# Attention over token chunks of 116 instead of 128 and 64, the first block of w_in in two halves, and a new written order of the first nineteen units

## The chip, the cores and the metric

The kernel runs on one core of one Trainium2 chip. The metric is the device time of one execution in microseconds. Each core has five engines that run their own instruction streams: TensorE (PE, with its weight loads PEld), VectorE (DVE), ScalarE (ACT), GpSimd (POOL) and SyncE (SP). SP issues most DMAs here; they run on 16 DMA engines.

## The reference

Two attentions and a feed-forward block. A short set of 32 packed queries `p` attends to 576 tokens; the result is the key and value of a second attention, whose output goes through a two-layer block with the activation `h * erf(softplus(h))`.

```python
batch, n_heads, seq, head_dim = (8, 8, 576, 64)      # 32 packed queries
def sm_attn(qq, kk, vv):
    s = scale * np.matmul(qq, kk.transpose(0, 1, 3, 2))
    s = s - np.max(s, axis=-1, keepdims=True)
    a = np.exp(s)
    a = a / (np.sum(a, axis=-1, keepdims=True) + 1e-09)
    return np.matmul(a, vv)
p_packed = sm_attn(p, k, v)
out = sm_attn(q, p_packed, p_packed)
# x: (4608, 512), heads side by side;  w_in: (512, 2048);  w_out: (2048, 512)
h = x @ w_in
sp = np.maximum(h, 0.0) + np.log1p(np.exp(-np.abs(h)))
g = h * erf(sp)
return (g @ w_out).astype(np.float32)
```

`w_in` and `w_out` arrive as 64-bit floats; the kernel takes their words apart itself.

## The kernel before

**Attention of a batch, `attention(b)`.** It is a generator: each `yield` ends a stage, and the caller decides where the next stage stands among the other work. The stages load `p` and four `k` tiles (line 233), then five `v` chunks of up to 128 tokens with all heads side by side (line 239: four of 128 rows and one of 64, 2,048 bytes a row), then four `q` tiles (244). First scores follow (252), their exponentials, the transposes of these token chunk by token chunk (`turn_chunks`, 267, and `turn_rest` for the last 64 tokens, 270), and the pooling `pool`, which multiplies each transposed chunk `a1t` with its chunk of `v` (277): two halves `r`, in each five chunks, in each four heads, so 40 products, which the trace counts as 80 matmuls. The pooled rows are normalised and transposed into `pt`. The second scores are `pt` against `q` (359), and their softmax over groups of 32 gives `a2`, kept as a high and a low part.

**The block.** The pooled values are multiplied into `w_in` once per batch: `w_prime(b, j)` (W, line 389) gives W' for the j-th 512 columns of `w_in`, in PSUM; `w_prime_high` (H on ScalarE, G on VectorE, 395) and `w_prime_low` (V, 400) keep it as two parts. A *unit* is 256 columns of the hidden layer for half a batch's tokens (288); there are 128 units. For each, `h_half` (h, 421) does six matmuls for 128 columns, `h_copy` takes them out of PSUM (c on ScalarE, d on VectorE, 429), `softplus` and `erf` (s, e) and `gate` (m, 443) form g, `split_high` (u on VectorE, U on ScalarE) and `split_low` (v) part it, and `o_part` (o, 472) multiplies with `w_out`; `put` (p, 481) writes results away.

**Weights.** A 512-column block of `w_in` is four tiles. `F j.c` issues the DMA of one of them (line 102, 4,096 bytes a row), `L j.c` writes the upper 16 bits (ScalarE, 108), `K j.c` merges the lower bits (VectorE, 112). `F f`, `L f`, `K f` do the same for a tile of `w_out`, and S or R (143) and T (146) split it. Staging tiles, `w_out` tiles and their splits share 18 buffers, tag `wo`.

**What sets the order.** The first part of the program is the string `BEGINNING`: words executed one after the other while the program is traced, and each engine's instructions (PE, DVE, ACT, SP) keep that order. `A`, `B` and `C` are the next stage of attention of batches 0, 1 and 2; `N` and `X` the next step of the second softmax of batch 0 for its first and second half of tokens; `i21` is 21 matmuls on an identity that keep PE's clock up. Units 0 to 3 and 4 to 7 belong to batch 0 (its two halves of tokens, first half of the hidden layer), 8 to 15 to batch 1, 16 to 19 to batch 0's second half of the hidden layer. From unit 20 a plan places the rest; attention of batch b+2 runs in pieces between the units of batch b.

Batch 0 has its own form (`roomy`): scores stay in PSUM, and `v` and `q` lie in buffers that are still free.

Of the kernel before, what the change touches and what calls it, by code (L numbers as in the profile page):

```python
# [26 lines left out]
BEGINNING = """
A A F0.2 F0.3 A F0.1 F0.0 i6 A A i9 A F3 F1.2 B F1.0 A A A F1.1 A F1.3 A A L0.2 K0.2 F2 A A A A A A A L0.1 L0.0 A F1
F2.1 A i21 N F5 N F0 N K0.1 B X N N L0.3 K0.3 N K0.0 N F7 N X F4 L1.2 K1.2 N N W0.0 H0.0 V0.0 B L3 B B B B X B L1.0 X
K1.0 h1.0 h1.1 c1.1 d1.0 F6 L1.1 K1.1 L1.3 K1.3 X h0.0 W0.1 G0.1 c0.0 L2 h0.1 V0.1 F2.0 d0.1 h3.0 h3.1 X X B B s1 X B  # L30
s0 e0 h2.0 e1 X X d2.0 h2.1 d2.1 d3.0 L0 L1 h4.0 h4.1 B c4.1 m0 K0 h5.0 h5.1 c5.0 L5 K1 B B d4.0 d5.1 s2 o0.3 K5 o0.2
L4 K3 c3.1 S0 m1 s3 o0.0 B s4 K2 e4 o1.0 L7 K4 B B e3 m4 R4 T0 K7 u4 m3 R1 T1 B B L6 K6 h6.0 h6.1 o0.1 o1.2 B B c6.1
o1.3 e2 m2 o1.1 c6.0 s5 B h7.0 h7.1 o2.0 S3 T3 o3.0 B B v4 R6 B e5 c7.1 S2 T2 B F8 o2.3 B c7.0 s7 o2.2 F2.2 L2.2 o3.3
p3.3 o2.1 o3.1 p3.1 p3.0 W1.0 o4.1 R7 s6 o4.3 B F3.1 L2.0 B B B B H1.0 o3.2 V1.0 F3.2 p3.2 m5 e7 o4.0 u5 v5 L2.1 K2.1
F2.3 L2.3 o4.2 h8.0 c8.0 m7 U7 K2.0 T7 F3.0 W1.1 G1.1 h9.0 c9.0 R5 T5 o5.3 K2.2 V1.1 T6 o5.0 K2.3 e6 m6 u6 T4 h8.1
o5.2 c8.1 s8 F11 h9.1 c9.1 s9 v6 o5.1 h10.0 c10.0 h10.1 c10.1 L3.0 F3.3 W0.2 v7 F9 s10 L8 e8 G0.2 V0.2 e10 m10 L3.2
L3.1 K3.1 m8 u8 v8 h11.0 h11.1 K3.2 L9 o6.0 o6.2 c11.1 e9 m9 c11.0 o6.3 o7.3 o6.1 F13 o7.1 o7.0 h12.0 h12.1 K3.0 o7.2
p7.1 L3.3 K3.3 u9 L11 v9 c12.0 p7.2 p7.0 h13.0 c12.1 s12 c13.0 s11 W0.3 G0.3 K8 h13.1 c13.1 F10 R8 T8 V0.3 o8.0 o9.0
o8.2 o9.2 o8.1 o9.1 p7.3 o8.3 s13 e13 F12 K9 S9 T9 e11 u10 m11 L10 h14.0 W1.2 v10 o10.2 K10 H1.2 S10 h14.1 V1.2 e12
d14.1 L12 o10.0 U11 F15 o9.3 T10 F14 c14.0 s14 K11 S11 v11 K12 R12 T12 W1.3 o10.1 H1.3 h15.0 T11 L14 h15.1 o10.3 o11.3  # L40
p11.3 m12 U12 c15.0 d15.1 s15 v12 o11.2 L13 o11.1 p11.1 o11.0 p11.0 h16.0 K14 K13 h16.1 c16.1 m13 S14 c16.0 s16 p11.2
R13 V1.3 u13 v13 e14 m14 o12.0 u14 h19.0 o12.1 d19.0 C T13 e15 v14 o12.3 o12.2 o13.2 h17.0 L15 e16 K15 o13.3 h17.1
c17.1 o13.0 C S15 d17.0 o13.1 o14.1 m15 s17 C h18.0 h18.1 u15 v15 C d18.0 h19.1 c19.1 T15 o14.3 s19 d18.1 o14.0 s18
e18 m16 e17 m17 T14 o14.2 e19 m19 C m18
"""


# [1 line left out]
def tile_pack_attention_moe(ctx: ExitStack, tc: tile.TileContext, qT, kT, v, pT, w_in, w_out, outT):  # L49
    nc = tc.nc  # L50
    P = 128
    B, _, NC, S = qT.shape
# [45 lines left out]
    def load_parts(src, name):

        n = src.shape[1]  # L100
        st = opool.tile([P, 4 * n + 2], U16, name=name, tag="wo")
        nc.sync.dma_start(st[:, 1:4 * n + 1], src.bitcast(U16))
        top = st[:, 2:4 * n + 2].bitcast(BF16).rearrange("p (n four) -> p n four", four=4)[:, :, 2]
        middle = st[:, 2:4 * n + 2].bitcast(U32).rearrange("p (n two) -> p n two", two=2)[:, :, 0]

        def land(dst):
            upper = dst.bitcast(F16).rearrange("p (n two) -> p n two", two=2)[:, :, 1]
            nc.scalar.copy(upper, top)  # L108

        def work(dst):  # L110
            bits = dst.bitcast(U32)
            nc.vector.scalar_tensor_tensor(bits, middle, 13, bits, op0=ALU.logical_shift_right, op1=ALU.bitwise_or)  # L112
# [87 lines left out]
    def attention(b):  # L200
# [34 lines left out]
        v_at = ("hs", "hs", "hs", "kvq", "kvq") if roomy else ("kvq",) * NCH  # L235
        values = [chunk(f"v{j}", v_at[j]) for j in range(NCH)]
        for j in range(NCH):
            n = min(P, S - j * P)
            nc.sync.dma_start(values[j][0:n, 0:2 * NC * 64], v[b, j * P:j * P + n, :])
# [31 lines left out]

        def pool(r, po):

            for j in range(NCH):
                n = min(P, S - j * P)
                for c in range(NC):
                    nc.tensor.matmul(po[NK * c:NK * c + NK, 64 * r:64 * r + 64],  # L277
                                     a1t[0:n, r, j, NK * c:NK * c + NK],
                                     values[j][0:n, 64 * (2 * c + r):64 * (2 * c + r) + 64],
                                     start=(r == 0 and j == 0), stop=(r == 1 and j == NCH - 1),  # L280
                                     skip_group_check=True)
# [101 lines left out]

    def w_prime(b, j):

        ps = ps_m.tile([P, 2, 512], F32, name=f"wp{b}_{j}", tag="ps_m")
# [4 lines left out]
        raw[b, j] = ps

    def w_prime_high(b, j, copy=nc.scalar.copy):
        hi = wpool.tile([P, 2, FB], F32R, name=f"wph{b}_{j}", tag="wph")
        copy(hi[:], raw[b, j][:])  # L395
        wp[b, j] = (hi, wpool.tile([P, 2, FB], F32R, name=f"wpl{b}_{j}", tag="wpl"))

    def w_prime_low(b, j):
# [1 line left out]
        nc.vector.tensor_tensor(lo[:], raw.pop((b, j))[:], hi[:], op=ALU.subtract)  # L400
# [301 lines left out]
```

## Time and profile before

| | |
|---|---|
| median of 3 runs | 734.68 us (734.39 to 735.19) |
| the profiled execution | 735.09 us |
| its span, first to last instruction | 733.3 us |
| granted TensorE clock, mean | 0.998 |
| PE, DVE, ACT busy | 98%, 75%, 78% of the span |
| moved by DMA | 58.42 MB |

A busy share is that of the whole span and mixes a start that waits for data with a long stretch in which PE has no gap; the stretches of time are therefore read one by one. A matmul's recorded time contains its way through the array, so sums of matmul times exceed what PE needs from start to start.

### The profile page before, as it was taken

The page shows a single profiled execution, that of the slowest core. Times are in us where ns is not written, and L with a number is a line of the kernel's source. Part 1 is how long each engine was busy: PE and PEld are TensorE (multiplying, and loading weights), DVE is VectorE, ACT ScalarE, POOL GpSimd, SP SyncE. Part 2 cuts the span into 40 slices and gives each one's busy share as a digit, 9 for nine tenths or more (in the row PEclk, how much of TensorE's full clock was granted, in tenths as well). Part 3 has the DMA queues.
Part 4 walks back from the last instruction along what each step waited for, and adds up shares of the span by engine and source line. Part 5 has one row for each costly group of instructions (what it writes and reads, how often), then busy time and mean ns, then how long its engine had stood idle before and what let it go on. Part 6 is the DMA issues. An engine that isn't in the chain of part 4 may idle for free.

```text
span 733.3 us, 15411 instructions
## 1 busy us (share of the span) xinstructions
PE 720.5 (98%) x6400; PEld 656.3 (89%) x6400; DVE 547.8 (75%) x831; ACT 573.0 (78%) x965; POOL 36.7 (5%) x56
## 2 busy tenths in 40 slices
...
GB/s 314 400 198 176 152 162 108 86 121 70 26 35 98 133 33 1 56 114 63 34 2 89 81 63 34 1 85 88 81 9 2 85 50 34 1 18 16 9 25 34
DMA packets 30279, 58.42 MB, mean 80 GB/s; under 512 B 3584, under 2 KB 12800, under 8 KB 30208
## 3 DMA queue, kind: packets, MB, share of 16 engines
...
## 4 chain that ended last, share of the span: by engine, by line
PE 88%; DMA 4%; DVE 4%; issue 1%; ACT 1%; SPq 0%; POOL 0%; POOLq 0%
PE o L472 54%; PE h L421 26%; PE wp L389 4%; DMA wos<-w_out 1%; PE p L277 1%; DMA wi<-w_in 1%; PE s L359 1%; PE s L252 1%; DMA k<-kT 1%; DMA v<-v 1%; PE t L267 1%; DVE gl L456 0%; DVE wohl L146 0%; DVE wpl L400 0%; ACT wo L108 0%
## 5 line engine op out<-in xcount | busy, mean ns | idle before, releaser
L472 PE MATMUL o<-gh,wohl 128*128 128x288 f32 x1984 | 422.7, 298 | 0.0
L472 PEld LDWEIGHTS o<-gh,wohl 128*128 128x128 f32 x1984 | 325.6, 188 | 13.7 <-issue 7.8
L472 PE MATMUL o<-gl,wohl 128*128 128x288 f32 x992 | 293.1, 296 | 0.1
L472 PEld LDWEIGHTS o<-gl,wohl 128*128 128x128 f32 x992 | 186.9, 188 | 0.9 <-DVE gl L456 0.4
L421 PE MATMUL h<-a2h,wph 128*128 128x288 f32 x512 | 154.3, 301 | 1.1 <-ACT hs L429 0.5
L421 PE MATMUL h<-a2h,wpl 128*128 128x288 f32 x512 | 151.6, 296 | 1.5 <-DVE wpl L400 1.5
L421 PE MATMUL h<-a2l,wph 128*128 128x288 f32 x512 | 151.0, 295 | 0.0
L431 ACT ACTIVATE hs<-h 128x288 f32<-128x288 f32 x192 | 77.9, 410 | 73.3 <-PE h L421 72.2
L519 DVE SCALAR_TENSOR_TENSOR hs<-t,hs 128x576 f32<-128x576 f32 x96 | 72.6, 756 | 62.6 <-ACT t L518 62.5
L421 PEld LDWEIGHTS h<-a2h,wph 128*128 128x128 f32 x512 | 96.1, 188 | 25.4 <-ACT u L515 8.4
L421 PEld LDWEIGHTS h<-a2h,wpl 128*128 128x128 f32 x512 | 96.0, 188 | 3.3 <-DVE wpl L400 2.4
L421 PEld LDWEIGHTS h<-a2l,wph 128*128 128x128 f32 x512 | 96.1, 188 | 0.9 <-issue 0.8
L456 DVE TENSOR_TENSOR gl<-hs,gh 128x576 fp32r<-128x576 f32 x124 | 93.5, 755 | 2.8 <-ACT gh L449 0.6
L518 ACT ACTIVATE t<-t,bias 128x576 f32<-128x576 f32 x96 | 74.0, 771 | 24.3 <-DVE t L517 24.3
L516 DVE SCALAR_TENSOR_TENSOR t<-t,hs 128x576 f32<-128x576 f32 x96 | 72.1, 751 | 17.3 <-ACT u L515 17.2
L449 DVE CAST gh<-hs 128x576 fp32r<-128x576 f32 x121 | 55.8, 461 | 31.3 <-PE o L472 28.1
L513 ACT ACTIVATE t<-hs,bias 128x576 f32<-128x576 f32 x96 | 74.6, 777 | 2.5
L515 ACT ACTIVATE u<-t,bias 128x576 f32<-128x576 f32 x96 | 74.5, 776 | 1.6
L514 ACT ACTIVATE t<-t,bias 128x576 f32<-128x576 f32 x96 | 74.2, 773 | 1.8
L517 DVE SCALAR_TENSOR_TENSOR t<-u,t 128x576 f32<-128x576 f32 x96 | 72.3, 753 | 1.4
L400 DVE TENSOR_TENSOR wpl<-wp,wph 128x1024 fp32r<-128x1024 f32 x32 | 38.8, 1211 | 7.0 <-ACT wph L395 6.2
L389 PE MATMUL wp<-w_in_sb,pt 64*32 64x512 f32 x512 | 37.1, 601 | 0.2 <-DVE w_in_sb L112 0.2
...
## 6 DMA issues: line engine op xcount, KB each, us to landing
k<-kT SPq DMA_DIRECT2D x32, 288.0 KB, 4.6
q<-qT SPq DMA_DIRECT2D x32, 288.0 KB, 4.2
v<-v SPq DMA_DIRECT2D x32, 256.0 KB, 3.6
wi<-w_in SPq DMA_DIRECT2D x16, 512.0 KB, 7.1
wos<-w_out SPq DMA_DIRECT2D x16, 512.0 KB, 6.5
...
v<-v SPq DMA_DIRECT2D x8, 128.0 KB, 4.0
```

Source lines behind the costliest of these rows:

```text
L389: nc.tensor.matmul(ps[NK * c:NK * c + NK, r, :], pt[b][64 * r:64 * r + 64, NK * c:NK * c + NK], w_in_sb[64 * r:64 * r + 64, c, j * FB:(j + ...
L421: nc.tensor.matmul(ps[:, 0:HT], w[:, r, fo:fo + P], a[:, r, c * HT:(c + 1) * HT], start=(m == 0), stop=(m == 5))
L431: nc.scalar.mul(dst, src, 0.5)
L456: nc.vector.tensor_tensor(glo[:], hs[:], ghi[:], op=ALU.subtract)
L472: nc.tensor.matmul(acc[b, c, d][:, 0:HT], w[f][:, d * P:(d + 1) * P], gg[:, k, :], start=(first and k == 0 and m == 0), stop=(last and k = ...
L513: nc.scalar.activation(t[:], hs[:], AF.Tanh, bias=bias[:, 0:1], scale=2.0 * T_SCALE)
L514: nc.scalar.activation(t[:], t[:], AF.Square, bias=bias[:, 1:2], scale=Q_SCALE)
L515: nc.scalar.activation(u[:], t[:], AF.Tanh, bias=bias[:, 2:3], scale=U_SCALE)
L516: nc.vector.scalar_tensor_tensor(t[:], t[:], 0.5 * A2, hs[:], op0=ALU.mult, op1=ALU.add)
L517: nc.vector.scalar_tensor_tensor(t[:], u[:], 0.5 * A1, t[:], op0=ALU.mult, op1=ALU.add)
L518: nc.scalar.activation(t[:], t[:], AF.Tanh, bias=bias[:, 3:4], scale=2.0 * A_SCALE)
L519: nc.vector.scalar_tensor_tensor(hs[:], t[:], 1.0, hs[:], op0=ALU.add, op1=ALU.mult)
```

## The change

Three things. First, the 576 tokens are cut into five chunks of nearly one size: four of 116 and one of 112. The loads of `v`, the transposes and `pool` go by these chunks; the transposed chunks keep their places, 128 columns apart. Second, block 0 of `w_in` can be loaded and used in two halves of 256 columns, named pieces 4 and 5: for batch 0, `F4.c`, `L4.c`, `K4.c`, `W0.4`, `H0.4`, `V0.4` and the same with 5 take the place of piece 0, with half the columns each. Both halves share one staging tile and one pair of W' tiles; a row of a half is 2,048 bytes. Batch 1 still forms W' of block 0 whole. Third, `BEGINNING` is written anew.

```diff
+    PIECES = [(j * FB, FB) for j in range(NFB)] + [(0, FB // 2), (FB // 2, FB // 2)]
-    NT = S // P
-    REM = S - NT * P
-    NCH = NT + 1
+    NCH = -(-S // P)
+    CH = -(-S // NCH // 4) * 4
+    NT = NCH - 1
+    REM = S - NT * CH
...
+    def load_w_in(j, c):
+        f0, n = PIECES[j]
+        dst, src = w_in_sb[:, c, f0:f0 + n], w_in[c * P:(c + 1) * P, f0:f0 + n]
...
+        if (f0 // FB, c) not in staged:
+            staged[f0 // FB, c] = staging(f"wi{j}_{c}", FB)
+        land, work = load_parts(staged[f0 // FB, c], src, f0 % FB)
...
-            n = min(P, S - j * P)
-            nc.sync.dma_start(values[j][0:n, 0:2 * NC * 64], v[b, j * P:j * P + n, :])
+            n = min(CH, S - j * CH)
+            nc.sync.dma_start(values[j][0:n, 0:2 * NC * 64], v[b, j * CH:j * CH + n, :])
...
-                nc.tensor.transpose(out[:, j * P:(j + 1) * P], a1[:, r, j * P:(j + 1) * P], ident[:])
+                nc.tensor.transpose(out[0:CH, j * P:(j + 1) * P], a1[:, r, j * CH:(j + 1) * CH], ident[:])
...
-            nc.tensor.transpose(out, a1[:, r, NT * P:S], ident[:])
+            nc.tensor.transpose(out, a1[:, r, NT * CH:S], ident[:])
...
-                n = min(P, S - j * P)
+                n = min(CH, S - j * CH)
...
-            nc.scalar.copy(a1t[:, :, 0:NT].rearrange("p r j k -> p r (j k)"), banks[:, :, 0:NT * P])
+            nc.scalar.copy(a1t[0:CH, :, 0:NT].rearrange("p r j k -> p r (j k)"), banks[0:CH, :, 0:NT * P])
...
+                nc.tensor.matmul(ps[NK * c:NK * c + NK, r, 0:n], pt[b][64 * r:64 * r + 64, NK * c:NK * c + NK],
+                                 w_in_sb[64 * r:64 * r + 64, c, f0:f0 + n], start=True, stop=True)
```

The start of the written order, before and after (the first three or so lines of each; F, L, K and A as above):

```diff
-A A F0.2 F0.3 A F0.1 F0.0 i6 A A i9 A F3 F1.2 B F1.0 A A A F1.1 A F1.3 A A L0.2 K0.2 F2 A A A A A A A L0.1 L0.0 A F1
-F2.1 A i21 N F5 N F0 N K0.1 B X N N L0.3 K0.3 N K0.0 N F7 N X F4 L1.2 K1.2 N N W0.0 H0.0 V0.0 B L3 B B B B X B L1.0 X
-K1.0 h1.0 h1.1 c1.1 d1.0 F6 L1.1 K1.1 L1.3 K1.3 X h0.0 W0.1 G0.1 c0.0 L2 h0.1 V0.1 F2.0 d0.1 h3.0 h3.1 X X B B s1 X B
+A A F5.2 F5.3 F4.2 A F4.1 F5.1 F4.0 F5.0 i6 A A A F4.3 i9 A A F3 F1.2 B F1.3 F1.0 F1.1 A A F2 A A A A L5.3 A L4.2 A A
+A K4.2 L5.2 K5.2 F5 A A L4.1 L5.1 F1 i21 A N F0 N N K5.1 K4.1 N N L4.0 F7 B L5.0 K4.0 L4.3 K4.3 W0.4 H0.4 N N N X V0.4
+K5.0 L1.2 N L3 K5.3 W0.5 B X B H0.5 B B B F4 N V0.5 h1.0 c1.0 L1.3 F2.1 K1.2 L1.0 h1.1 B L1.1 X X c1.1 h0.0 K1.0 K1.1
+K1.3 X W0.1 G0.1 F6 V0.1 c0.0 L2 h0.1 X h3.0 h3.1 d0.1 F2.0 X B B s1 B s0 e0 X X X h2.0 c2.0 h2.1 d2.1 d3.0 L0 B e1
```

In these lines the second `A` loads `v` of batch 0 and the third `A` its `q`; the first `B` loads `k`, the second `v` and the third `q` of batch 1. The rest of the string holds the same kinds of words in another order; over all of it, four more `h` copies stand on VectorE (17 d in place of 13), two fewer whole high parts of W' (2 G in place of 4), and one or two splits of `w_out` and of g changed engine.

More of the change, by code (lines that the diff above doesn't have):

```diff
@@ L27 @@
 BEGINNING = """
-A A F0.2 F0.3 A F0.1 F0.0 i6 A A i9 A F3 F1.2 B F1.0 A A A F1.1 A F1.3 A A L0.2 K0.2 F2 A A A A A A A L0.1 L0.0 A F1
-F2.1 A i21 N F5 N F0 N K0.1 B X N N L0.3 K0.3 N K0.0 N F7 N X F4 L1.2 K1.2 N N W0.0 H0.0 V0.0 B L3 B B B B X B L1.0 X
-K1.0 h1.0 h1.1 c1.1 d1.0 F6 L1.1 K1.1 L1.3 K1.3 X h0.0 W0.1 G0.1 c0.0 L2 h0.1 V0.1 F2.0 d0.1 h3.0 h3.1 X X B B s1 X B
-s0 e0 h2.0 e1 X X d2.0 h2.1 d2.1 d3.0 L0 L1 h4.0 h4.1 B c4.1 m0 K0 h5.0 h5.1 c5.0 L5 K1 B B d4.0 d5.1 s2 o0.3 K5 o0.2
-L4 K3 c3.1 S0 m1 s3 o0.0 B s4 K2 e4 o1.0 L7 K4 B B e3 m4 R4 T0 K7 u4 m3 R1 T1 B B L6 K6 h6.0 h6.1 o0.1 o1.2 B B c6.1
@@ L33 @@
[L33 to L42, printed above, removed]
@@ L43 @@
-c17.1 o13.0 C S15 d17.0 o13.1 o14.1 m15 s17 C h18.0 h18.1 u15 v15 C d18.0 h19.1 c19.1 T15 o14.3 s19 d18.1 o14.0 s18
-e18 m16 e17 m17 T14 o14.2 e19 m19 C m18
+A A F5.2 F5.3 F4.2 A F4.1 F5.1 F4.0 F5.0 i6 A A A F4.3 i9 A A F3 F1.2 B F1.3 F1.0 F1.1 A A F2 A A A A L5.3 A L4.2 A A
+A K4.2 L5.2 K5.2 F5 A A L4.1 L5.1 F1 i21 A N F0 N N K5.1 K4.1 N N L4.0 F7 B L5.0 K4.0 L4.3 K4.3 W0.4 H0.4 N N N X V0.4
+K5.0 L1.2 N L3 K5.3 W0.5 B X B H0.5 B B B F4 N V0.5 h1.0 c1.0 L1.3 F2.1 K1.2 L1.0 h1.1 B L1.1 X X c1.1 h0.0 K1.0 K1.1
@@ new lines @@
+K1.3 X W0.1 G0.1 F6 V0.1 c0.0 L2 h0.1 X h3.0 h3.1 d0.1 F2.0 X B B s1 B s0 e0 X X X h2.0 c2.0 h2.1 d2.1 d3.0 L0 B e1
+h4.0 L1 K0 h4.1 m0 h5.0 L5 B B d4.0 d4.1 s4 h5.1 c5.1 K1 o0.3 K3 K5 B s2 o0.2 L4 S0 d3.1 K2 s3 e4 m1 o1.2 e3 o0.0 o0.1
+o1.0 K4 B d5.0 B L7 m4 T0 K7 m3 R1 T1 B B L6 K6 h6.0 c6.0 h6.1 R4 c6.1 e2 S6 B B o1.1 m2 o1.3 B h7.0 h7.1 o2.0 S3 s5
+u4 e5 T3 B B v4 B R2 c7.1 T2 B B o2.3 o2.1 c7.0 s7 F2.2 o2.2 o3.3 L2.2 p3.3 s6 o3.1 p3.1 o3.0 p3.0 F3.1 B W1.0 H1.0 B
+B B R7 F3.2 L2.0 o3.2 p3.2 m5 U5 o4.3 V1.0 B v5 F2.3 K2.2 o4.0 e7 o4.1 L2.3 o4.2 W1.1 h8.0 d8.0 F3.0 m7 L2.1 K2.1 H1.1
@@ new lines @@
+V1.1 U7 e6 F8 m6 h9.0 d9.0 R5 o5.2 T5 o5.0 h8.1 o5.3 K2.3 K2.0 u6 c8.1 s8 h9.1 c9.1 T4 h10.0 c10.0 o5.1 s9 h10.1 v6
+c10.1 W0.2 T6 v7 L3.2 K3.2 F11 s10 F9 e10 L8 e8 L3.0 T7 G0.2 V0.2 m8 u8 L3.1 v8 h11.0 h11.1 c11.0 o6.2 d11.1 K8 K3.1
+o6.1 F13 e9 K3.0 L9 o6.0 o7.0 o6.3 o7.3 o7.1 h12.0 h12.1 K9 p7.0 o7.2 F3.3 L3.3 L11 K3.3 m9 u9 v9 c12.1 c12.0 p7.2
+h13.0 s12 s11 F12 W0.3 H0.3 h13.1 F10 m10 d13.0 d13.1 S8 T8 o8.2 o8.0 o9.0 p7.1 o8.1 s13 o9.1 h14.0 V0.3 S9 T9 o9.2
+e13 e11 m11 u10 p7.3 o8.3 L10 W1.2 K10 v10 L12 H1.2 o9.3 S10 V1.2 h14.1 d14.1 o10.0 e12 u11 F15 T10 F14 v11 K12 c14.0
@@ L45 @@
+s14 K11 R11 R12 o10.1 W1.3 H1.3 o11.0 h15.0 L14 T12 h15.1 o10.3 L13 o11.1 p11.1 o11.3 p11.3 T11 m12 U12 d15.1 d15.0
+s15 o10.2 h16.0 p11.0 h16.1 c16.1 o11.2 p11.2 K14 m13 v12 d16.0 s16 K13 R14 R13 u13 v13 o12.0 C e14 o12.1 h19.0 d19.0
+V1.3 T13 m14 e15 U14 m15 v14 L15 o12.3 K15 h17.0 h17.1 c17.1 e16 o12.2 o13.3 o13.0 o13.1 C h19.1 c19.1 S15 T15 o14.1 C
+h18.0 h18.1 c17.0 s17 c18.1 C o13.2 m16 o14.2 s19 c18.0 s18 e18 T14 U15 v15 e17 m17 e19 m18 m19 C o14.3 o14.0
 """
@@ L96, in tile_pack_attention_moe, with staging, load_parts @@
         nc.vector.memset(bias[:, i:i + 1], c)
[L98 to L104, printed above, removed]
+    def staging(name, n):
+        return opool.tile([P, 4 * n + 2], U16, name=name, tag="wo")
+    def load_parts(st, src, n0):
+        n1 = n0 + src.shape[1]
+        nc.sync.dma_start(st[:, 4 * n0 + 1:4 * n1 + 1], src.bitcast(U16))
+        words = st[:, 4 * n0 + 2:4 * n1 + 2]
+        top = words.bitcast(BF16).rearrange("p (n four) -> p n four", four=4)[:, :, 2]
+        middle = words.bitcast(U32).rearrange("p (n two) -> p n two", two=2)[:, :, 0]
         def land(dst):
@@ L114, in load_parts @@
         return land, work
-    def load_f32(dst, src, name):
-        if src.dtype == F32:
+    staged = {}
+    def load_w_in(j, c):
+        f0, n = PIECES[j]
+        dst, src = w_in_sb[:, c, f0:f0 + n], w_in[c * P:(c + 1) * P, f0:f0 + n]
+        if w_in.dtype == F32:
             nc.sync.dma_start(dst, src)
             return (lambda: None,) * 2
-        land, work = load_parts(src, name)
+        if (f0 // FB, c) not in staged:
+            staged[f0 // FB, c] = staging(f"wi{j}_{c}", FB)
+        land, work = load_parts(staged[f0 // FB, c], src, f0 % FB)
         return (lambda: land(dst)), (lambda: work(dst))
-    def load_w_in(j, c):
-        return load_f32(w_in_sb[:, c, j * FB:(j + 1) * FB], w_in[c * P:(c + 1) * P, j * FB:(j + 1) * FB], f"wi{j}_{c}")
     def load_w_out(f):
+        src = w_out[f * P:(f + 1) * P, :]
         if w_out.dtype == F32:
             wo[f] = opool.tile([P, DM], F32, name=f"wo{f}", tag="wo")[:]
-            return load_f32(wo[f], w_out[f * P:(f + 1) * P, :], f"wos{f}")
-        land, work = load_parts(w_out[f * P:(f + 1) * P, :], f"wos{f}")
+            nc.sync.dma_start(wo[f], src)
+            return (lambda: None,) * 2
+        land, work = load_parts(staging(f"wos{f}", DM), src, 0)
         def begin():
@@ L306, in attention @@
                 yield
-                copy(a1t[:, r, 0:NT].rearrange("p j k -> p (j k)"), turned[r][:, 0:NT * P])
+                copy(a1t[0:CH, r, 0:NT].rearrange("p j k -> p (j k)"), turned[r][0:CH, 0:NT * P])
                 copy(a1t[0:REM, r, NT], rest[0:REM, 0:P])
@@ L384, in w_prime @@
     def w_prime(b, j):
+        f0, n = PIECES[j]
         ps = ps_m.tile([P, 2, 512], F32, name=f"wp{b}_{j}", tag="ps_m")
```

16 lines of the change are left out of this document (9 added, 7 removed).

## The prediction, before the changed kernel was built

> **What bounds the kernel now.** I read the page first (busy shares, DMA issues), then busy time by stretches, then the chain of waits and the order of events of the first 60 us, last the pooling of one steady batch.
>
> ```profile
> span 733.3 us, 15411 instructions
> PE 720.5 (98%) x6400; PEld 656.3 (89%) x6400; DVE 547.8 (75%) x831; ACT 573.0 (78%) x965; POOL 36.7 (5%) x56
> ...
> q<-qT SPq DMA_DIRECT2D x32, 288.0 KB, 4.2
> v<-v SPq DMA_DIRECT2D x32, 256.0 KB, 3.6
> wi<-w_in SPq DMA_DIRECT2D x16, 512.0 KB, 7.1
> ...
> v<-v SPq DMA_DIRECT2D x8, 128.0 KB, 4.0
> ```
> ```profile
> core 0: us, PE busy (x) PEld busy (x) DVE busy (x) ACT busy (x) POOL busy (x), PEclk, DMA share, GB/s
> 0.00:10.00 10.00, 5.20 (x52) 4.33 (x53) 4.87 (x10) 1.28 (x1) 4.17 (x8) 1.00 0.80 258
> 10.00:20.00 10.00, 8.14 (x143) 5.88 (x142) 4.88 (x14) 3.79 (x13) 0.00 (x0) 0.92 1.03 385
> 20.00:30.00 10.00, 9.01 (x90) 6.59 (x88) 9.12 (x17) 7.03 (x13) 1.05 (x2) 0.91 1.04 397
> 30.00:40.00 10.00, 8.45 (x59) 5.81 (x58) 9.30 (x17) 9.29 (x16) 1.05 (x2) 1.00 1.04 383
> 40.00:50.00 10.00, 10.00 (x133) 8.60 (x132) 8.97 (x19) 9.55 (x16) 1.79 (x3) 1.00 0.66 248
> 50.00:60.00 10.00, 10.00 (x79) 7.39 (x78) 8.30 (x15) 9.49 (x15) 0.77 (x1) 1.00 0.06 8
> ...
> 300.00:400.00 100.00, 100.00 (x909) 91.84 (x910) 77.50 (x117) 81.12 (x142) 0.00 (x0) 1.00 0.20 62
> ```
>
> There are two regimes. From about 80 us TensorE is never idle (100.00 of 100 us in 300 to 400), so a microsecond taken off PE there comes off the end. Before that PE starts little (52 to 143 matmuls in 10 us): DMA is saturated from 10 to 40 us (1.03, 385 GB/s), and from 20 us VectorE and ScalarE are over nine tenths busy. What arrives later there starts everything later.
>
> **The order of the start.**
>
> ```profile
> 3.07 2.58 SPq L239 DMA_DIRECT2D v<-v  x5
> 7.79 2.66 SPq L244 DMA_DIRECT2D q<-qT  x4
> ```
> ```profile
> 4.50 6.59 DMA v<-v
> ```
> ```profile
> DMA to landing us min/median/max: 7.0/7.1/7.3
> ```
> ```profile
> SPq L244 <- DMA v<-v: 1.3, 3, 0.7
> ```
> ```profile
> 13.31 1.73 PE L277 MATMUL p<-v,a1t 128*32 128x64 f32 x80
> 14.76 0.69 DVE L112 SCALAR_TENSOR_TENSOR w_in_sb<-wi,w_in_sb 128x512 uint32<-128x512 uint32 x1 [1.54 <-ACT w_in_sb L108]
> 16.02 0.29 DVE L344 TENSOR_TENSOR a<-p,sm 128x128 f32<-128x128 f32 x1
> 17.05 1.24 PE L359 MATMUL s<-q,pt 64*32 64x288 f32 x32 [0.35 <-ACT pt L351]
> 17.89 0.85 DVE L174 STREAM_TRANSPOSE ta<-s 128x288 f32<-128x288 f32 x2 [1.57 <-PE s L359]
> 21.23 0.78 ACT L108 CAST w_in_sb<-wi 128x512 f16<-128x512 bf16 x1 [0.53 <-DMA wi<-w_in]
> 24.79 0.75 DVE L187 TENSOR_TENSOR ta<-ta,mx 128x576 f32<-128x576 f32 x1
> 28.22 1.22 DVE L400 TENSOR_TENSOR wpl<-wp,wph 128x1024 fp32r<-128x1024 f32 x1
> 29.50 0.40 PE L421 MATMUL h<-a2h,wpl 128*128 128x288 f32 x1 [0.73 <-DVE wpl L400]
> ```
>
> These are, in this order: SP's issues, a piece of the chain of waits, the landing time of q's four transfers, SP's waits of the first 24 us, and the timeline. The fourth v chunk is issued at 4.50 and lands at 11.09. q lands 7.0 to 7.3 us after its issue, the last of which begins at 10.1 (7.79 + 2.66 less one issue), so it is complete at 17.1 to 17.4, beside the second scores at 17.05. The last piece of w_in's first block lands at 21.2 (ScalarE waits for it). From 17.89 VectorE works nearly without a gap to the low half of W' at 29.44, which releases the matmul at 29.50.
>
> **The change part by part.**
>
> *Pooling on TensorE (gain).* One steady batch, loads alone:
>
> ```profile
> 235.12 1.73 PE L277 MATMUL p<-v,a1t 128*32 128x64 f32 x80
> 236.78 0.40 PE L472 MATMUL o<-gl,wohl 128*128 128x288 f32 x1
> ```
> ```profile
> 235.11:235.55 0.44, 0.43 (x32) 1.00 0.00 0
> 235.55:235.69 0.14, 0.06 (x5) 1.00 0.00 0
> 235.69:235.80 0.11, 0.10 (x8) 1.00 0.00 0
> 235.80:235.94 0.14, 0.06 (x8) 1.00 0.00 0
> ```
>
> Pooling lasts 1.66 us from its first start to that of the next matmul. In each half of it 32 loads of the 128-row form go in 0.44 us (0.11 per eight), then nothing new starts for 0.14 us until the array works in the 64-row form, eight go in 0.11, and again 0.14 pass. With chunks of 116 and 112 rows all ten sets have the long form (more than 64 rows don't fit the short one). Three of the four pauses go; the last, into the 128*128 matmuls, stays: 3 x 0.135 = 0.40 us a batch. Ends: 0 if every change of chunk pauses, 0.42. Six steady batches: 2.4 us off the end. Batches 0 and 1 lie in the start, where other work decides, so their 0.4 is not counted. The transposes keep their number, and the rest's (now 112 wide) its 128 moving columns: 0, at most 0.05 us a batch.
>
> *Loads of v (loss).* A chunk is 128 rows of 2,048 bytes, eight to each of 16 DMA engines; the 64-row chunk is four each and lands no sooner (4.0 against 3.6 us). 116 = 4 x 29 has no equal share for 16. No row shows such a transfer. Bounds: shares of eight and seven, as the 128-row row (cost 0); or equal shares on four engines, 29 rows each. (One engine would have no reason, since four divides.) The ends are far apart. I take the equal deal, because each transfer in this trace divides by 16 and none shows an uneven one; both ends stay in the range. The Trainium skill, "DMA: Bandwidth & Descriptors", section "Why a DMA increments its semaphore by 16 and not by 1", says that a transfer runs on the largest number of engines, up to 16, that divides the slowest dimension of both sides: four for 116, all 16 for 112. No run here shows it yet; by that rule the sum is the one that follows, without it the first rival's.
>
> One engine's rate is 385 / 16 = 24.1 GB/s. The busiest four carry 4 x 29 + 7 = 123 rows of v instead of 36: 87 x 2,048 bytes = 178 KB, 7.4 us. All that is queued after v on these four is late by that. v is complete near 11.5 + 7.4 = 18.9 instead of before the pooling at 13.31; pooling's second half (0.6) and the 2.0 us from its end at 15.04 to 17.05 give 21.5. q comes later: it goes behind three half pieces of w_in (768 KB, before 1,024: 0.7 us less), so 17.2 + 7.4 - 0.7 = 23.9. The second scores thus start 6.8 us late. The last half piece lands near 21.2 + 7.4 = 28.6; it is cast and merged by 29.4, and behind it on VectorE stand, up to W0.5's low part, five operations over 576 elements (0.75 to 0.85 each), a small reciprocal (0.4), two half merges and two half low parts (priced below), 6.6 us: 36.0, while 23.9 + 12.4 (17.05 to 29.44) gives 36.3. Both say 6.6 us after 29.44. The queue throttles further: each transfer waits for the landing of the one eight before it (q waits for v three times above), so q is issued one piece per late v chunk; it stays ahead of its place on the four engines, so I add 0. Idle PE can't make it up: VectorE and ScalarE are the limit until 80 us, and their work has only moved.
>
> *v of batch 1.* The same 7.4 us again.
>
> ```profile
> L277 PE MATMUL p<-v,a1t x80: 216/219/243, 47.7 to 49.3; 128*32 128x64 f32 x64, 64*32 64x64 f32 x16
> L239 SPq DMA_DIRECT2D v<-v x5: 328/328/471, 28.3 to 33.6; - x5
> ...
> DMA to landing us min/median/max: 7.8/8.9/10.2
> ```
>
> Landed by 43.8 at most, needed at 47.7. After: 43.8 + 14.8 = 58.6 against 47.7 + 6.6 = 54.3, so up to 4.3 us more; 0 if the landing is nearer the median and DMA's free time (0.66 and 0.06 in 40 to 60) takes it up. I take 2.3. The next batches are covered, and without cover would cost 7.4 each:
>
> ```profile
> L277 PE MATMUL p<-v,a1t x80: 216/219/243, 149.4 to 150.9; 128*32 128x64 f32 x64, 64*32 64x64 f32 x16
> L239 SPq DMA_DIRECT2D v<-v x3: 328/367/477, 131.3 to 132.2; - x3
> ```
>
> 17 us lie between issue and use.
>
> *Halves.* Four more DMAs, ScalarE casts and VectorE merges, one more W' with its high and low copy. VectorE: 0.75 us at 576 elements, 0.29 at 128, so 1.02 ns each and 0.16 fixed; a half merge is 0.42 against 0.69, a half low part 0.70 against 1.22. Between second scores and first finished W' there were three merges of block 0, one of block 1 and one low part (3 x 0.69 + 0.68 + 1.22 = 3.97); now six half merges and two half low parts (3.92). Equal: 0; ends -0.3 and +0.8, the latter if the four extra casts of ScalarE (0.78 whole, some 0.2 of it fixed) lie on the path. K0.2, which delayed pooling's sums (14.76 to 15.45), is split and stands elsewhere: under the late v, nothing.
>
> *Order.* On SP's queue F7 now goes ahead of batch 1's v and F2.1 behind its q (512 KB each: they cancel, 1.4 us either way). On the engines four `h` copies, two block copies and some splits change between ScalarE and VectorE, about 2 us in all; both are full from 20 to 80 us. I take 0, ends -1.5 and +1.5.
>
> **The sum.** Profiled execution 735.09 us (span 733.3 and 1.8 around it), which is 0.4 over the median of 734.68: 735.1 + 6.6 + 2.3 - 2.4 = 741.6, against the median 741.2; I say 741.
>
> **Rivals.**
> 1. *The 116 rows go to all 16 engines.* Then nothing is late, q even 0.6 earlier (three half pieces ahead of it instead of two whole ones), and the pauses' 2.4 us remain: 734.7 - 2.4 - 0.6 = 731.7 (730.4 to 733.2 with the order's ends). For it: the 64-row rows give no hint of a worse deal; against it: 116 / 16 is no whole number. It decides if v is complete by about 16 us. Faster.
> 2. *The start is late, but batch 1's v costs its full 4.3 us and ScalarE's half casts and the order 1.5 more:* 734.7 + 6.6 + 4.3 + 1.5 - 2.4 = 744.7. For it: 9.3 to 9.6 us of ScalarE's 10 in 30 to 50; against it: DMA's pause after 50 us.
> 3. *The late start is mostly absorbed*, because the new order does other work meanwhile: 2.4 us of loss would be left to cancel the gain, 734.7. Against it: that work needs the same late w_in pieces.
>
> **Numbers.** Equal shares on four engines with the cost as summed 0.60, rival 2 0.10, rival 1 0.25, rival 3 0.05. Likeliest case's own range: 737.3 (5.0 us at the start, none at batch 1) to 743.5. Since the faster case holds 0.25, the range goes to it: 730.5 to 745. A measurement tells 0.2% (1.5 us) from no change: faster 0.25, same 0.05, slower 0.70.
>
> **What would show it.** v's 116-row transfers of batch 0 land 3 to 8 us later than 11.1 and one after the other, some 2.4 us apart; pooling of batch 0 starts or ends near 19, second scores near 24, the first matmul with W' low near 36; GB/s in 10 to 20 us falls far under 385 while something still waits for DMA. A steady pooling lasts about 1.26 us with 128*32 forms alone. If v lands by 11 to 12 us, the forecast is wrong by its largest term; if pooling still takes 1.6, by its gain.

## The result

The changed kernel takes 745.21 us (median of 4 runs, 744.92 to 745.32), the kernel before 734.93 us beside it on the same chip: a ratio of 1.014, 95% interval 1.0122 to 1.0157. The change costs 10.3 us. The forecast was 741.0 with a range up to 745.0: the direction and the main mechanism were right, the size was 4.2 us short, and the time lies 0.2 us above the range.

First the page of the changed kernel: its span, the busy time, and the group of v's issues.

```profile
span 743.4 us, 15448 instructions
...
PE 721.6 (97%) x6416; PEld 657.2 (88%) x6416; DVE 545.1 (73%) x835; ACT 575.6 (77%) x971; POOL 36.2 (5%) x56
...
v<-v SPq DMA_DIRECT2D x32, 232.0 KB
```

The busy times are those of before within 3 us on every engine, so the 10 us are almost all waiting. Busy time by stretches (PE, PEld, DVE, ACT, POOL, then granted clock, DMA share, GB/s) says where:

```profile
10.00:20.00 10.00, 4.72 (x57) 3.04 (x55) 2.15 (x9) 2.79 (x10) 0.00 (x0) 0.78 0.72 200
20.00:30.00 10.00, 9.19 (x113) 6.39 (x114) 5.05 (x11) 4.16 (x10) 0.00 (x0) 0.71 0.95 313
30.00:40.00 10.00, 6.59 (x94) 4.80 (x93) 9.85 (x21) 6.87 (x15) 0.53 (x1) 1.00 1.02 400
40.00:50.00 10.00, 8.77 (x63) 6.59 (x64) 8.69 (x17) 9.37 (x16) 1.05 (x2) 1.00 0.75 256
50.00:60.00 10.00, 7.29 (x107) 5.79 (x106) 5.71 (x11) 5.23 (x9) 1.79 (x3) 0.83 0.85 263
...
300.00:400.00 100.00, 100.00 (x906) 92.60 (x902) 78.17 (x115) 80.38 (x136) 0.00 (x0) 1.00 0.15 49
```

From 10 to 20 us DMA moves 200 GB/s where it moved 385, while five chunks of v are waited for; VectorE works 2.15 of those 10 us (4.88 before), and the granted TensorE clock is 0.78 and then 0.71 (0.92 and 0.91 before). From 50 to 60 us the same comes again for batch 1: 5.71 against 8.30 on VectorE, and the clock falls to 0.83. The steady stretch has no gap, as before.

The start in the timeline (start, duration, idle time before it and what ended that; PEld is TensorE's weight load):

```profile
13.60 0.43 PE L286 MATMUL p<-v,a1t 116*32 116x64 f32 x16
16.80 0.44 PE L286 MATMUL p<-v,a1t 116*32 116x64 f32 x8 [2.77 <-DMA v<-v]
19.18 0.44 PE L286 MATMUL p<-v,a1t 116*32 116x64 f32 x8 [1.93 <-DMA v<-v]
20.04 1.51 PE L286 MATMUL p<-v,a1t 112*32 112x64 f32 x48 [0.42 <-DMA v<-v]
22.80 3.64 PE L368 MATMUL s<-q,pt 64*32 64x288 f32 x32 [0.36 <-ACT pt L360]
24.02 0.18 PEld L368 LDWEIGHTS s<-q,pt 64*32 64x32 f32 x4 [0.58 <-DMA q<-qT]
25.95 0.85 DVE L183 STREAM_TRANSPOSE ta<-s 128x288 f32<-128x288 f32 x2 [2.37 <-PE s L368]
35.96 0.69 DVE L416 TENSOR_TENSOR wpl<-wp,wph 128x512 fp32r<-128x512 f32 x1
36.71 0.40 PE L437 MATMUL h<-a2h,wpl 128*128 128x288 f32 x1
```

Two chunks are there at 13.60; the next two come at 16.80 and 19.18, 2.4 us apart, and the last, of 112 rows, at 20.04. The second scores start at 22.80 (17.05 before), VectorE begins on them at 25.95 (17.89), the first matmul with the low half of W' at 36.71 (29.50). The same for batch 1:

```profile
53.37 0.43 PE L286 MATMUL p<-v,a1t 116*32 116x64 f32 x16
53.95 0.32 PE L286 MATMUL p<-v,a1t 116*32 116x64 f32 x8 [0.15 <-DMA v<-v]
56.50 0.41 PE L286 MATMUL p<-v,a1t 116*32 116x64 f32 x8 [2.23 <-DMA v<-v]
57.24 1.51 PE L286 MATMUL p<-v,a1t 112*32 112x64 f32 x48 [0.33 <-DMA v<-v]
58.68 7.44 PE L488 MATMUL o<-hs,wo 128*128 128x288 f32 x20
```

The 20 `o` matmuls take 7.44 us here. In the kernel with chunks of 112 below they take 5.29. That row, and not only the waits above it, is what the forecast lacked. The pooling of a steady batch, last:

```profile
246.88 1.33 PE L286 MATMUL p<-v,a1t 116*32 116x64 f32 x80
248.13 0.40 PE L488 MATMUL o<-gl,wohl 128*128 128x288 f32 x1
```

From its first start to the next matmul 1.25 us pass, where before there were 1.66, and only the long array form is left.

### The profile page after: what moved, and what is told of

Its sections match the earlier page's. It is cut to its first block, busy times and chain, and to the rows that moved or that the text cites. A ratio compares the mean times of both kernels' runs of the same rounds, so it can differ in the third digit from the quotient of the medians.

```text
span 743.4 us, 15448 instructions
## 1 busy us (share of the span) xinstructions
PE 721.6 (97%) x6416; PEld 657.2 (88%) x6416; DVE 545.1 (73%) x835; ACT 575.6 (77%) x971; POOL 36.2 (5%) x56
## 4 chain that ended last, share of the span: by engine, by line
PE 93%; DMA 4%; DVE 2%; SPq 1%; ACT 0%; issue 0%
PE o L488 56%; PE h L437 27%; PE wp L399 5%; DMA v<-v 4%; PE s L368 2%; PE p L286 1%; PE s L261 1%; PE t L276 1%; DVE w_in_sb L117 0%; SPq L248 0%; SPq L242 0%; DVE ta L183 0%; DVE mx L185 0%; DVE ta L187 0%; DVE m L299 0%; PE p L279 0%
## 5 line engine op out<-in xcount | busy, mean ns | idle before, releaser
L534 ACT ACTIVATE t<-t,bias 128x576 f32<-128x576 f32 x96 | 74.0, 771 | 23.9 <-DVE t L533 23.8
L416 DVE TENSOR_TENSOR wpl<-wp,wph 128x1024 fp32r<-128x1024 f32 (+1 forms) x33 | 38.9, 1179 | 7.1 <-ACT wph L412 6.2
L399 PE MATMUL wp<-w_in_sb,pt 64*32 64x512 f32 (+1 forms) x528 | 37.5, 588 | 3.6 <-DVE w_in_sb L117 3.6
```

The source lines that it names most:

```text
L399: nc.tensor.matmul(ps[NK * c:NK * c + NK, r, 0:n], pt[b][64 * r:64 * r + 64, NK * c:NK * c + NK], w_in_sb[64 * r:64 * r + 64, c, f0:f0 + n ...
L534: nc.scalar.activation(t[:], t[:], AF.Tanh, bias=bias[:, 3:4], scale=2.0 * A_SCALE)
```

## Experiments

All times are medians beside the kernel before, which took 734.7 to 735.1 us in these comparisons; ratios are to it, with their 95% intervals.

### Which part of the change costs

**Chunks of 112.** The changed kernel with four chunks of 112 rows and one of 128, which both divide by 16.

```diff
-    CH = -(-S // NCH // 4) * 4
+    CH = 112
...
-            n = min(CH, S - j * CH)
+            n = CH if j < NT else REM
...
```

> The changed kernel with four chunks of 112 tokens and one of 128, all else as changed (halves, new order). Theory D (the deal: a v transfer runs on as many DMA engines as divide its rows, so 116 rows on four): all chunks divide by 16, batch 0's chunks land near 11 us as before the change, pooling of a steady batch stays at 1.26 us, total 731 us (730 to 733), PE's losses before 150 us at or under those of the kernel before. Rival O (the loss comes from the new order and the halves): over 742 us, second scores still near 23 us.

Measured 732.3 us, ratio 0.9964 (0.9951 to 0.9976): 12.9 us less than with 116, from four rows a chunk. The pooling and second scores of batch 0, and pooling of batch 1 with the `o` matmuls behind it, in its timeline:

```profile
13.88 1.40 PE L286 MATMUL p<-v,a1t 112*32 112x64 f32 x80
16.38 1.57 PE L368 MATMUL s<-q,pt 64*32 64x288 f32 x32 [0.35 <-ACT pt L360]
...
46.58 1.33 PE L286 MATMUL p<-v,a1t 112*32 112x64 f32 x80
47.84 5.29 PE L488 MATMUL o<-hs,wo 128*128 128x288 f32 x20
```

No wait for v stands before either pooling. This version beats both kernels.

**The kernel before with 116.** Its own order and whole pieces of w_in, chunks of 116 and 112.

```diff
-    NT = S // P
-    REM = S - NT * P
-    NCH = NT + 1
+    NCH = -(-S // P)
+    CH = 116
+    NT = NCH - 1
+    REM = S - NT * CH
...
```

> The kernel before, its order and whole w_in blocks kept, with chunks of 116 and 112 only. Theory D: v lands 2.4 us apart, second scores near 23.5 us, pooling of batch 1 waits for v again: 741 to 746 us. Rival O: 732.3 us, since only the pauses of steady pooling go.

Measured 747.43 us, ratio 1.0174 (1.0161 to 1.0188): the chunk alone brings the whole loss, 2.2 us more than in the new order and 1.4 us above what either theory allowed; why more was not taken apart.

**The kernel before with 112.** The same, with one number more.

```diff
-    CH = 116
+    CH = 112
```

> The kernel before with chunks of 112 and 128 only. Both theories: steady pooling 1.26 us in place of 1.66, six batches, so 734.8 - 2.4 = 732.4 us; another 0.4 if batch 0's shorter pooling counts at the start (731.9 to 732.6). If it is over 733.5, the gain of the pauses is partly lost again.

Measured 733.04 us, ratio 0.9974 (0.9963 to 0.9984): the pooling's gain alone, about 2 us.

**Halves and order alone.** The changed kernel with the old chunks of 128 and 64.

```diff
-    CH = -(-S // NCH // 4) * 4
+    CH = 128
...
```

> The changed kernel (halves and new order) with the chunks of the kernel before, 128 and 64. Theory D: the order and the halves are worth little, 733.3 to 735.5 us, pooling 1.66 us again. Rival O: 745.2 + 2.4 = 747.6 us.

Measured 734.31 us, ratio 0.9993 (0.9984 to 1.0002): with chunks that arrive in time, the two halves and the new order are worth nothing that can be measured.

### What 116 does to a load

**117 and 118 rows.** The same edit as for 112 with `CH = 117` and `CH = 118`: 117 = 13 x 9 and 118 = 2 x 59. If the rows are dealt out in equal shares, 117 goes to 13 engines and 118 to 2.

> The changed kernel with chunks of 117 tokens and one of 108. 117 = 13 x 9, 108 = 12 x 9. Theory D (equal shares on the largest number of engines up to 16 that divides the rows): 45 rows of v on the busiest engine instead of 36, so 0.8 us more per batch and no visible wait: 732 to 734 us, though 117 is no multiple of 16 nor even. Rival M (any transfer whose rows are no multiple of 16 is slow): 745 us or more.

> The changed kernel with chunks of 118 tokens and one of 104. 118 = 2 x 59. Theory D: two engines, 59 rows each, 4.9 us a chunk; busiest engine 249 rows instead of 36, that is 18 us late per early batch where 116 gave 7.4: 755 to 772 us, batch 0's chunks landing 4.9 us apart. Rival M: like 116, 745 us.

Measured 732.51 us (0.9971; 0.9961 to 0.998) with 117, 763.67 us (1.0397; 1.0376 to 1.0418) with 118. One row more than 116 removes the loss, two rows more make it more than twice as large. The pooling of batch 0, first with 117, then with 118:

```profile
13.77 1.40 PE L286 MATMUL p<-v,a1t 117*32 117x64 f32 x80
```
```profile
17.20 0.44 PE L286 MATMUL p<-v,a1t 118*32 118x64 f32 x8 [3.00 <-DMA v<-v]
23.26 0.44 PE L286 MATMUL p<-v,a1t 118*32 118x64 f32 x8 [5.62 <-DMA v<-v]
28.67 0.44 PE L286 MATMUL p<-v,a1t 118*32 118x64 f32 x8 [4.97 <-DMA v<-v]
```

Chunks of 118 arrive 5.4 to 6.1 us apart, those of 116 2.4 us apart. With equal shares that is 59 x 2,048 bytes in 5.4 to 6.1 us and 29 x 2,048 in 2.4 us: an estimate of 20 to 22 and of 25 GB/s for one engine, beside the 24.1 that the forecast took. That is the rule of the Trainium skill, "DMA: Bandwidth & Descriptors", section "Why a DMA increments its semaphore by 16 and not by 1", which the prediction cited without a run behind it; these three sizes agree with it.

**116 rows, loaded as 112 and 4.** Pooling computes on 116 rows, and each load is split into two DMAs.

```diff
-            nc.sync.dma_start(values[j][0:n, ...], v[b, j * CH:j * CH + n, :])
+            for r0, r1 in ((0, 112), (112, n)):
+                if r1 > r0:
+                    nc.sync.dma_start(values[j][r0:r1, ...], v[b, j * CH + r0:j * CH + r1, :])
```

> The changed kernel, chunks of 116 kept in all computation, but each 116-row load issued as one of 112 rows and one of 4 rows (the 112-row chunk whole). Theory D: busiest engine 39 rows; nine transfers a batch instead of five take places among the eight in flight, worth at most 2 us at the start: 732 to 735 us. Rival P (products, transposes or copies over 116 partitions are slow by themselves): 745 us.

Measured 733.18 us, ratio 0.9982 (0.9973 to 0.9992). The loss goes although pooling still works on 116 rows: it lies in the transfer, not in TensorE.

### Which batch pays

The chunk is 116 for some batches and 112 for the others:

```diff
+        CH = 116 if b == 0 else 112      # in the other two kernels b > 1 and b == 1
+        REM = S - NT * CH
...
```

> Chunks of 116 and 112 for batch 0 alone, 112 and 128 for all others, halves and order as changed. Theory D with the first term as measured: 732.3 + 7 to 9 = 739 to 741.5 us, first use of W' low near 36.7 us, no wait for v in batch 1's pooling. If the two early batches hide one another: under 736.

Batch 0 alone: 738.89 us, ratio 1.0059 (1.0043 to 1.0076), 6.6 us over the kernel with 112.

> Chunks of 116 and 112 for batches 2 to 7, 112 and 128 for batches 0 and 1. Theory D with the cover claimed in the prediction (17 us between issue and use): no cost, 731.5 to 733 us, equal to the kernel with 112 and 128. If each of the six batches costs its 7.4 us: over 770 us.

Batches 2 to 7 alone: 732.13 us, 0.996 (0.9946 to 0.9974): no cost, the 17 us between issue and use cover it.

> Chunks of 116 and 112 for batch 1 alone. If the terms add: 732.3 + 3.5 to 5 = 735.8 to 737.3 us, with the start as in the 112 kernel and a wait in batch 1's pooling or for the w_out tile queued behind v. If DMA's free time after 50 us covers it, as the lower end of the prediction had it: 732 to 733.5 us.

Batch 1 alone: 737.59 us, ratio 1.0039 (1.0024 to 1.0054), 5.3 us over the kernel with 112 and above what either theory allowed. This is where the forecast failed. The timeline of TensorE (pooling, the `o` matmuls, the second half of the second scores), and the granted clock (the column behind POOL) in four stretches of it:

```profile
49.04 0.32 PE L288 MATMUL p<-v,a1t 116*32 116x64 f32 x8 [2.12 <-DMA v<-v]
49.80 0.88 PE L288 MATMUL p<-v,a1t 112*32 112x64 f32 x48 [0.44 <-DMA v<-v]
50.61 6.81 PE L490 MATMUL o<-hs,wo 128*128 128x288 f32 x20
...
62.30 0.72 PE L370 MATMUL s<-q,pt 64*32 64x288 f32 x16 [0.41 <-DVE ta L378]
```
```profile
50.00:51.00 1.00, 1.00 (x49) 0.91 (x40) 0.00 (x0) 0.00 (x0) 0.00 (x0) 0.89 1.07 255
51.00:52.00 1.00, 1.00 (x3) 0.68 (x2) 0.00 (x0) 0.00 (x0) 0.00 (x0) 0.50 0.96 367
...
53.00:54.00 1.00, 1.00 (x3) 0.68 (x2) 0.00 (x0) 0.24 (x1) 0.00 (x0) 0.50 0.54 209
54.00:55.00 1.00, 1.00 (x5) 0.83 (x4) 0.44 (x1) 1.00 (x2) 0.00 (x0) 0.91 0.26 107
```

Pooling waits 2.6 us in all. Then the clock is 0.50 for about 3.4 us (from 51 to 54 us, and some 0.2 us on either side, by the means 0.89 and 0.91), and 20 `o` matmuls take 6.81 us where 5.29 were enough. Beside it VectorE and ScalarE do nothing from 50 us until ScalarE starts near 53.8: ScalarE's next word, L4, takes the tile of w_out whose DMA, F4, stands on SP's queue behind v and q of batch 1. It waits 5.5 us for it, and the second half of the second scores waits 0.41 us for what is behind that. Two suspects, then, besides the bare wait.

### What batch 1's wait sets off

**The w_out tile ahead of v.** F4 issued before batch 1's v, first with 116 for batch 1 alone, then in the changed kernel.

```diff
-L4.0 F7 B L5.0 ... H0.5 B B B F4 N V0.5
+L4.0 F7 F4 B L5.0 ... H0.5 B B B N V0.5
```

> 116 rows a chunk for batch 1 alone, and the w_out tile of word F4 issued ahead of batch 1's v instead of behind its v and q. Theory F (the tile carries much of the loss, because ScalarE waits 5.5 us for it in program order and everything behind that waits too): that wait is gone, what is left is pooling's own 2.1 us wait for v, so 734.0 to 735.5 us against 737.6 with the tile behind. Theory V (the late v itself carries it, and the tile's lateness is beside it): ScalarE's wait is gone, but the time stays at 737.0 to 738.0. A third way: v is now 0.7 us (one tile of 256 KB at 385 GB/s) later, pooling waits that much longer and the time is 738 or more.

> The changed kernel (116 rows in every batch) with the w_out tile of word F4 issued ahead of batch 1's v. Theory F: the tile's part of batch 1's loss, 2 to 3.5 us, goes, so 741.5 to 743.2 us against 745.2; the start's 6.6 us and pooling's own wait remain. Theory V: 744.6 to 745.8, no change that can be measured.

Measured 738.57 us (1.0055; 1.0038 to 1.0072) and 747.23 us (1.0169; 1.0154 to 1.0184): not better; the medians are 1 and 2 us higher, with intervals that still overlap those without the move. The first is the third way of its expectation, with the tile mis-sized: it is 512 KB and not 256, 1.4 us at 385 GB/s. The tile's wait is gone, but v is issued 1.4 us later and pooling ends 2.5 us later than without the move, and ScalarE now stands still for the pooled rows instead. So one wait was taken away and the other made longer, and what the tile costs by itself these two runs can't tell. The waits of the first (total, times, longest), and one line of its chain of waits:

```profile
ACT pt L362 <- PE p L358: 7.4, 1, 7.4
PEld p L288 <- DMA v<-v: 5.6, 3, 2.7
```
```profile
36.99 14.60 DMA v<-v
```

**TensorE kept busy in the wait.** Products of the identity with itself, which nobody reads, ahead of the fourth chunk's products in batch 1's pooling; everything else is left as it is. First with 116 for batch 1 alone, then in the changed kernel.

```diff
             for j in range(NCH):
+                if b == 1 and r == 0 and j == 3:
+                    for _ in range(18):
+                        nc.tensor.matmul(pr[:, 2 * P:3 * P], ident[:], ident[:], start=True, stop=True)
```

> 116 rows a chunk for batch 1 alone, and 18 products of the identity with itself (about 0.11 us each, 2.0 us in all, read by nobody) ahead of the products of the fourth v chunk in batch 1's pooling, where TensorE waits 2.1 us anyway. Theory C (the standing engine is granted half its clock for some us afterwards, and that is what the forecast lacked): no stretch at 0.50 after the pooling, the 20 o matmuls behind it take 5.3 us in place of 6.8, and the time falls by 1.5 us, 737.6 to 736.1 (735.6 to 736.6). Theory W (only the wait counts): 737.6 or a little more, since the work is added and the wait stays.

> The changed kernel with the same 18 products of the identity at the same place in batch 1's pooling. Theory C: the 20 o matmuls take 5.3 us in place of 7.3, and the last 48 products of the pooling, which ran at half clock too, some 0.6 us less: 745.2 falls to 742.5 (742.0 to 743.3). Theory W: 745.2 or a little more.

Measured 737.14 us (1.0036; 1.0024 to 1.0048) and 745.17 us (1.014; 1.0124 to 1.0155): no gain that can be told, against theory C. Yet what C says of the clock came true. The timeline of the first of them, and the piece of its chain of waits in which the tile is waited for:

```profile
46.66 4.29 PE L289 MATMUL p<-ident 128*128 128x128 f32 x36
50.87 0.99 PE L291 MATMUL p<-v,a1t 116*32 116x64 f32 x56
51.80 5.12 PE L493 MATMUL o<-hs,wo 128*128 128x288 f32 x20
...
62.22 0.72 PE L373 MATMUL s<-q,pt 64*32 64x288 f32 x16 [0.50 <-DVE ta L381]
```
```profile
42.95 10.59 DMA wos<-w_out
```

The `o` matmuls take 5.12 us, and the second half of the second scores still starts at 62.22, since it now waits for the path through the w_out tile. The products were also mis-sized: each counts as two matmuls, so they lasted 4.3 us in place of 2.0 and pooling ended 1.2 us later than without them.

**Pooling moved behind two more `o` parts**, in the changed kernel and, as a control, with chunks of 112.

```diff
-K5 B s2 o0.2 L4 S0 d3.1 K2 s3 e4 m1 o1.2 e3
+K5 s2 o0.2 L4 S0 d3.1 K2 s3 e4 m1 o1.2 B e3
```

> The changed kernel with batch 1's pooling moved behind two more o parts (8 matmuls, 1.9 us at full clock) in the written order. Its waits for v, 2.7 us in all, should fall to 0.8 us, too short to cost the clock if theory C holds: 745.2 - 1.9 - 2.1 to 2.7 = 740.6 to 741.2. Theory W: 745.2 - 1.9 = 743.3. If the pooled rows are then late for the second scores, the gain is given back there, as in the control.

> Control: chunks of 112 and 128 rows, no late v, with the same move of batch 1's pooling. There is no wait to remove, so any change against 732.3 us is what the later pooling costs by itself: 732.3 (731.7 to 733.0) if the three o parts left behind it still cover the normalising and turning of the pooled rows; 733 to 734.5 if the second scores are then late.

Measured 745.93 us (1.0148; 1.0133 to 1.0164) and, for the control, 733.51 us (0.9974; 0.9963 to 0.9984). The control's interval overlaps that of the kernel with 112, and the medians lie 1.2 us apart, so the move costs little by itself. In the changed kernel the wait for v falls to 0.21 us, and TensorE then waits for the pooled rows to be normalised:

```profile
64.48 0.48 PE L356 MATMUL p<-ident,a 128*128 128x128 f32 x1 [2.34 <-DVE a L353]
```

The wait has moved and not gone, and the halved clock has moved with it (a mean of 0.74 from 65 to 70 us); which of the late pieces holds VectorE there was not taken apart.

**Both at once.** The tile is issued between v and q, so that v isn't made later, and 9 products in place of 18 fill the wait.

```diff
-L4.0 F7 B L5.0 ... H0.5 B B B F4 N V0.5
+L4.0 F7 B F4 L5.0 ... H0.5 B B B N V0.5
...
+                    for _ in range(9):
```

> 116 rows a chunk for batch 1 alone; the w_out tile of word F4 issued between batch 1's v and q; and 9 products of the identity (2.1 us; each is two matmuls in the trace, 36 took 4.2 us) in pooling's wait. Theory B (two parallel limits: pooling's wait with the half clock behind it, and the tile for which ScalarE waits; either alone makes 737.4): both are gone, pooling's bare wait of 2.6 to 3.0 us is left, so 732.3 + 2.6 to 3.0 = 734.9 to 735.4. Theory T (a third thing carries it): 737.0 to 738.0, as after each cure alone.

> The changed kernel with the same two cures for batch 1. Theory B: the 20 o matmuls behind the pooling take 5.1 us in place of 7.3 and no wait for the tile is left, so 745.2 - 2.2 to 2.8 = 742.4 to 743.0; the start's 6.6 and pooling's bare wait remain. Theory T: 744.6 to 745.8.

Measured 735.22 us with 116 for batch 1 alone (1.0006; 0.9996 to 1.0015) and 743.28 us in the changed kernel (1.0114; 1.0098 to 1.0129). The first is what two parallel limits gave, and its interval lies clear of the 1.0024 to 1.0054 without the cures; it leaves a third carrier no more than the 0.7 us by which its time is uncertain. The second has the same direction, 1.9 us where 2.2 to 2.8 were expected, and its interval touches that of the changed kernel by 0.0007. The timeline of the first:

```profile
47.02 2.27 PE L289 MATMUL p<-ident 128*128 128x128 f32 x18
49.33 0.32 PE L291 MATMUL p<-v,a1t 116*32 116x64 f32 x8
50.02 0.88 PE L291 MATMUL p<-v,a1t 112*32 112x64 f32 x48 [0.36 <-DMA v<-v]
50.83 5.12 PE L493 MATMUL o<-hs,wo 128*128 128x288 f32 x20
...
60.35 0.71 PE L373 MATMUL s<-q,pt 64*32 64x288 f32 x16
```

The second half of the second scores starts at 60.35 instead of 62.30, with no wait; the `o` matmuls start 3.0 us later than with chunks of 112 (50.83 against 47.84), and nothing more is lost behind them. So batch 1's 5.3 us are 2.9 of bare wait (735.2 - 732.3) and 2.4 that two paths of about one length held together: the half clock behind the wait, and the w_out tile behind the late transfers. By the rows of batch 1 alone the tile's path ends 0.41 us behind TensorE's own, the wait before 62.30. How the 2.4 would split if only one were cured cleanly stays open: the first cure of the tile also delayed v, and the first cure of the clock also lasted too long.

## Why the prediction was right, and where it failed

**v's transfers, right.** The step was arithmetic on 116 = 4 x 29, against the rival of 16 engines. The trace before held no such transfer, so no row could decide it; 0.75 (all cases but that rival) against 0.25 was a bet, and it held. Chunks come 2.4 us apart as forecast, and the sizes 117 and 118 show that the divisor decides.

**The start, right in size, by steps that partly cancel.** Forecast 6.6 us, measured 6.6 (batch 0 alone against chunks of 112); that they agree to a tenth is luck. q was to end the second scores' wait at 23.9; they started at 22.80, as soon as the pooled rows were there, so v held their start. But then their weight loads waited for q three times, 1.4 us in all, and they ran at half clock, a cost that no term held: by the means of 10 to 30 us the clock was at 0.50 for 10.2 us (4.4 and 5.8), where the kernel before has 3.4. So VectorE began on them at 25.95, 1.2 us later than 23.9 gives (24.7, with the 0.84 between the two rows of before). Behind that all but 0.4 us was made up: 36.71, where this branch gave 36.3 (6.9 us late, and not the 6.6 that the prediction reads from it). The other branch named, w_in's last half piece merged and 6.6 us of VectorE behind it, gave 36.0 for the first use of the low half of W', measured 36.71.

**Batch 1's v, the step that failed.** The prediction bounded it by 0 and 4.3 us and took 2.3, and the bounds were those of pooling's wait alone. That wait was about as taken (2.6 us of idle time, 2.9 in the end), but the term is 5.3 us: no price stood there for what follows a wait. The prediction named what is queued behind v on the four DMA engines, and not what stands behind it in two instruction streams: TensorE's next 20 matmuls, of which the first part runs at half clock, and ScalarE's L4, whose tile's DMA, F4, lay behind v and q on SP's queue. Even the upper bound was too low for it.

An earlier reading of the prediction stood in the way. It had TensorE without idle time only from about 80 us, and starting little before that, 52 to 143 matmuls in 10 us; but the steady stretch has 91, and its own rows for 40 to 60 us have PE at 10.00 of 10. (ScalarE, on the other hand, is at 7.03 of 10 from 20 to 30 us and not over nine tenths.) In the kernel with chunks of 112 the chain of waits stays on TensorE from this piece to 80 us, where the view ends:

```profile
38.21 1.61 PE h L437 x10
```

Batch 1's pooling lies behind that point, so what TensorE loses there, by waiting or by half clock, comes off the end.

**Rival 2, near in number only.** Its 744.7 us lies 0.5 from the measured time, but it was reached with 4.3 us for batch 1 and 1.5 for ScalarE's half casts and the order. The halves and the order cost nothing (0.9993), and batch 1 more than its 4.3.

**Both batches together, a smaller miss.** 6.6 and 5.3 make 11.9; the whole is 12.9. In the changed kernel the clock stays at 0.50 about twice as long as with batch 1 alone, 6.8 us (0.4 of the two before 57, by their mean of 0.90, then six whole ones, and 0.4 of the next):

```profile
55.00:57.00 2.00, 0.41 (x8) 0.18 (x8) 0.71 (x2) 0.26 (x1) 0.00 (x0) 0.90 0.85 280
57.00:58.00 1.00, 0.76 (x31) 0.76 (x34) 0.00 (x0) 0.00 (x0) 0.00 (x0) 0.50 0.85 189
...
63.00:64.00 1.00, 1.00 (x4) 0.72 (x4) 0.52 (x2) 0.99 (x2) 0.27 (x1) 0.79 0.20 78
```

The last 48 matmuls of pooling then go in 1.44 us (57.24 to 58.68) where 0.81 was enough (49.80 to 50.61), and the `o` matmuls in 7.44 in place of 6.81: 0.6 each, 1.2 for the missing 1.0. That was read from rows and not tried by itself.

**Pooling's gain, right.** 0.40 us a batch forecast, 0.41 in the rows (1.66 to 1.25), and 2.4 us for six batches beside the 2.6 that the kernel with 112 gains. **Halves and order at 0, right:** 0.9993. **Later batches covered, right:** 732.13.

With batch 1 at its measured price, and 1.0 for both together, the sum would be 735.1 + 6.6 + 5.3 + 1.0 - 2.4 = 745.6, beside 745.14 of the profiled execution. The three prices are differences between runs, so this sum tests only the gain.
